# Reordering the opening of a two-branch kernel: tile 3 transposed between two half ups, its root before two gate copies, the v of tile 1 copied earlier, tile 0 normalised in two halves

## The chip, the cores and the metric

The kernel runs on one core of a Trainium2 chip. The metric is the device time of one execution in microseconds (us); the time of a kernel is the median of several executions. The engines of the core run side by side, each through its own instructions in a fixed order: TensorE (PE in the profile, with its weight loads as PEld), VectorE (DVE), ScalarE (ACT), GpSimd (POOL) and SyncE (SP), which issues the transfers.

## The reference

A token block `x` of 2048 rows and 512 columns is normalised row by row, and two branches are computed from the normalised `xn` and added to `x`:

```
xn = layernorm(x)
# branch A: linear attention, 32 heads of 16, feature map softmax(+p), softmax(-p)
q, k, v = split(xn @ wqkv)
phi_q, phi_k = features(q @ w_phi), features(k @ w_phi)
kv, z = sum over tokens of phi_k x v, sum of phi_k
A = ((phi_q @ kv) / (phi_q @ z + 1e-6)) @ wo
# branch B: gated product, F = 1792
B = ((xn @ w_gate) * (xn @ w_up)) @ w_down
out = x + A + B
```

All inputs and the output are bf16; sums are float.

## The kernel before, in words

Tokens are cut into 16 tiles of 128, and the tiles into 4 groups of 4. Everything that multiplies needs the normalised tokens transposed (columns on partitions): `xnT`, four chunks of 128 columns. From there on TensorE carries the work: v, k and q products per tile (`proj`, line 249), the gate and up products of branch B per chunk f of 128 of the 1792 hidden columns and per group (`half`, line 280; `unit`, line 297), the sums over phi_k and v (`kv`), the attention output (`attend`), and the last products `fin`. The order on each engine is written out by hand: every engine runs its instructions in the order in which the program issues them, and waits at each one for what it reads and for the buffer it writes.

The change touches the opening, lines 348 to 386, which handles the first four tiles while the weights still arrive. For a tile n of these four:

- `ln_sums(n)` (line 160): VectorE takes the statistics of the row block, once its load has landed.
- `first_std(n, ...)` (line 338): VectorE aggregates them to mean and variance (line 339), ScalarE takes the root of the variance (line 341).
- `first_apply(n)` (line 343): VectorE inverts the root (line 345) and normalises the tile (line 178, in `ln_apply`).
- `lt(n)` (line 217): TensorE transposes the tile in four pieces (line 223) into one PSUM bank (tile 0: two banks), and ScalarE copies the bank to `xnT` in two halves (line 226). `proj` reads the chunks of `xnT` in order, so it can begin behind the first half.
- `proj(pv, n, wv)`: the v product, and `vcopy(n, ...)` (line 332) moves it to SBUF, on ScalarE for tiles 0 and 1, on VectorE for 2 and 3.

Between them stand gate and up products of the first two hidden chunks for tokens 0 to 255 only (tiles 0 and 1, `2 * P` columns): g of chunks 0 and 1, then u of chunks 0 and 1. `gate_copy` (line 287) moves a gate product to SBUF on ScalarE, and `hidden` (line 292) multiplies it with the up product on VectorE. After tile 3's v product the second halves of these chunks follow (tokens 256 to 511), then full units.

PSUM results come from a pool of six banks that are handed out in turn (`bank`, line 155): a product that takes a bank waits until the bank's last reader is through. The v products of tiles 0 and 1 have banks of their own. `warm_up` (line 325) issues matmuls on constants whose result nobody reads: nine of 512 columns and one of 256 at the start, one of 512 between the transposes of tile 0 and the first v product.

SyncE issues all loads of the opening in one list (lines 84 to 101), ahead of everything else: x of tiles 0 and 1, wv in two parts, x of tile 2, gate weights of chunks 0 and 1, x of tile 3, up weights of chunks 0 and 1, and on.

Of the kernel before, what the change touches and what calls it, by code (L numbers as in the profile page):

```python
# [11 lines left out]
ALU = mybir.AluOpType  # L12
# [9 lines left out]
def kernel(  # L22
# [12 lines left out]
    nc = tc.nc  # L35
    P = 128
    S, D = A_x.shape[-2], A_x.shape[-1]
# [25 lines left out]
    xall = xpool.tile([P, NT, D], BF16)  # L63
# [44 lines left out]
    def table(func, i):  # L108
        nc.scalar.activation(out=first[:, i:i + 1], in_=ones[:, 0:1], func=func, scale=1.0)
# [45 lines left out]
    def bank(name, dt=F32, n=TT):  # L155
        return ps_s.tile([P, n], dt, name=name, tag="s")
# [3 lines left out]
    def ln_sums(n):  # L160
        stats = lnpool.tile([P, nc.vector.BN_STATS_DIM], F32, name="stats")
        nc.vector.bn_stats(out=stats[:], in_=xall[:, n, :])  # L162
        return stats
# [9 lines left out]
        nc.gpsimd.tensor_tensor(out=rstd[:, 0:k], in0=ve[:, 0:k], in1=mhalf[:, 0:k], op=ALU.pow)  # L173
        return rstd

    def ln_apply(n, mean, rstd):
        xn = xnpool.tile([P, D], BF16, name="xn")
        nc.vector.tensor_scalar(out=xn[:], in0=xall[:, n, :], scalar1=mean, scalar2=rstd,
                                op0=ALU.subtract, op1=ALU.mult)
        xns[n] = xn  # L180

    def mv_tile():
        return lnpool.tile([P, GT, nc.vector.BN_AGGR_DIM], F32, name="mv", bufs=GT)
# [33 lines left out]
    def lt(n, nbanks=1):  # L217
        step = DC // nbanks
        tps = []
        for lo in range(0, DC, step):  # L220
            tp = bank("tp", BF16).rearrange("p (c t) -> p c t", c=DC)
            for c in range(lo, lo + step):
                nc.tensor.transpose(out=tp[:, c, :], in_=xns[n][:, c * P:(c + 1) * P], identity=ident[:])  # L223
            tps.append(tp)
        for lo in range(0, DC, 2):
            nc.scalar.copy(out=xnT[:, lo:lo + 2, n * P:(n + 1) * P], in_=tps[lo // step][:, lo:lo + 2, :])  # L226
# [3 lines left out]
    def make_bd():  # L230
        bo, wp = BO[:], wphi[:]
        nc.vector.tensor_tensor(out=bd[:], in0=_bcast_ap(bo, [bo.ap[0], [0, DC], [E1, 8], [1, DH]]),
                                in1=_bcast_ap(wp, [wp.ap[0], [DH, DC], [0, 8], [1, DH]]), op=ALU.mult)
# [15 lines left out]
    def proj(ps, n, w, js=range(DC)):  # L249
        for j in js:  # L250
            nc.tensor.matmul(ps, lhsT=xnT[:, j, n * P:(n + 1) * P], rhs=w[:, j, :],  # L251
                             start=(j == 0), stop=(j == DC - 1))
# [27 lines left out]
    def half(w, name, T, f, lo, hi):  # L280
        ps = bank(name)[:, 0:hi - lo]
        for c in range(DC):
            nc.tensor.matmul(ps, lhsT=w[:, c, f * P:(f + 1) * P], rhs=xnT[:, c, T * TT + lo:T * TT + hi],  # L283
                             start=(c == 0), stop=(c == DC - 1))
        return ps

    def gate_copy(ps, n):
        g_sb = gpool.tile([P, TT], BF16, name="g_sb")
        nc.scalar.copy(out=g_sb[:, 0:n], in_=ps)  # L289
        return g_sb  # L290

    def hidden(T, f, ps, g_sb, lo, hi):
        if T not in hTs:
            hTs[T] = hpool.tile([P, FC, TT], BF16, name="hT", tag="h")
        nc.vector.tensor_tensor(out=hTs[T][:, f, lo:hi], in0=ps, in1=g_sb[:, 0:hi - lo], op=ALU.mult)  # L295
# [29 lines left out]
    def warm_up(k, n=TT):  # L325
        for _ in range(k):
            nc.tensor.matmul(warm[:, 0:n], lhsT=ones[:, 0:P], rhs=ones[:, 0:n], start=True, stop=True)  # L327
# [4 lines left out]
    def vcopy(n, ps, copy=nc.scalar.copy):  # L332
        copy(out=vts[n % NV][:, :, :, 0:DH], in_=ps.rearrange("p (a b c) -> p a b c", a=8, b=4))  # L333

    mvs = [mv_tile() for n in range(GT)]
    stds = {}

    def first_std(n, stats):
        nc.vector.bn_aggr(out=mvs[n][:, 0, :], in_=stats[:])
        stds[n] = lnpool.tile([P, 1], F32, name="std", bufs=GT)  # L340
        nc.scalar.activation(out=stds[n][:], in_=mvs[n][:, 0, 1:2], func=AF.Sqrt, bias=epst[:], scale=1.0)

    def first_apply(n):
        rstd = lnpool.tile([P, 1], F32, name="rs1", bufs=GT)
        nc.vector.reciprocal(out=rstd[:], in_=stds[n][:])
        ln_apply(n, mvs[n][:, 0, 0:1], rstd[:])

    with tc.tile_pool(name="ps_v", bufs=1, space=PSUM) as ps_v:
        pv = [ps_v.tile([P, D], F32, name=f"pv{n}") for n in range(2)]
        first_std(0, ln_sums(0))  # L350
        stats = ln_sums(1)
        first_apply(0)
        first_std(1, stats)
        first_apply(1)
        lt(0, nbanks=2)
        warm_up(1)
        proj(pv[0][:], 0, wv, range(2))
        lt(1)
        proj(pv[0][:], 0, wv, range(2, DC))
        proj(pv[1][:], 1, wv)  # L360
        first_std(2, ln_sums(2))
        first_apply(2)
        vcopy(0, pv[0])
        g = [half(wg, "g", 0, 0, 0, 2 * P)]
        lt(2)
        g.append(half(wg, "g", 0, 1, 0, 2 * P))
        pv2 = bank("pv")
        proj(pv2, 2, wv)
        stats = ln_sums(3)
        g_sb = [gate_copy(g[0], 2 * P)]  # L370
        first_std(3, stats)
        first_apply(3)
        g_sb.append(gate_copy(g[1], 2 * P))
        vcopy(1, pv[1])
        u0 = half(wu, "u", 0, 0, 0, 2 * P)
        hidden(0, 0, u0, g_sb[0], 0, 2 * P)
        vcopy(2, pv2, nc.vector.tensor_copy)
        u1 = half(wu, "u", 0, 1, 0, 2 * P)
        hidden(0, 1, u1, g_sb[1], 0, 2 * P)
        lt(3)  # L380
        pv3 = bank("pv")
        proj(pv3, 3, wv)
        make_bd()
        vcopy(3, pv3, nc.vector.tensor_copy)
        table(AF.Exp, 1)
        nc.gpsimd.tensor_tensor(out=M4[:], in0=BO[:, 0:4, :], in1=BO[:, 4:8, :], op=ALU.add)
# [141 lines left out]
```

## Time and profile before

| | |
|---|---|
| median of 3 executions | 222.68 us (222.62 to 222.80) |
| the profiled execution, own time | 222.58 us |
| its span in the profile | 220.9 us |
| TensorE busy | 216.7 us (98%), 1309 matmuls |
| VectorE, ScalarE, GpSimd busy | 138.7, 89.4, 68.8 us |
| HBM read, written | 8.67 MB, 2.10 MB |

The span runs from the first instruction to the last; what lies around it is part of the time but not of the trace. In the views by time a row has the start and the length of a run of like instructions, in us from the start of the span, then engine, line, operation, what it writes and reads, and in brackets how long the engine stood idle before it and what ended that. Matmuls overlap: a row ends when the last result is out, some time after the array could take the next one, so the pace is read from start to start. In the view by stretches the columns are the stretch and its length, busy time and number of instructions for PE, PEld, DVE, ACT and POOL, then the granted clock of TensorE, the share of the DMA engines and their GB/s. In the view by groups the last column is busy time in us and the mean length of one in ns, then the idle time before.

### The profile page before, as it was taken

What the parts mean: (1) busy time and instruction counts of PE and PEld (TensorE: products, weight loads), DVE (VectorE), ACT (ScalarE), POOL (GpSimd) and SP (SyncE); (2) the same over time, 40 slices, a digit from 0 to 9 for tenths busy, and PEclk for the clock granted to TensorE, in tenths of its full rate; (3) what the DMA queues carried; (4) which work ended last, traced back from release to release, by engine and by line L of the source; (5) the groups of instructions that cost most, each with busy time, mean ns of one, the idle gap of its engine ahead of it and who ended that gap; (6) DMA issues with size and microseconds to landing.
All of it is one profiled execution on the core that took longest, in us unless ns stands there. A gap on an engine that the chain in (4) does not pass through costs nothing.

```text
span 220.9 us, 3515 instructions
## 1 busy us (share of the span) xinstructions
PE 216.7 (98%) x1309; PEld 104.7 (47%) x1309; DVE 138.7 (63%) x241; ACT 89.4 (40%) x170; POOL 68.8 (31%) x54
## 2 busy tenths in 40 slices
PE   8999999999999999999999999999999999999994
PEld 3554444445444444444444444444444444454443
DVE  4657986785569785757489964097645745444321
ACT  3665575449764885546353221231322323100000
POOL 3000455546335653637333643024033033000000
PEclk9999999999999999999999999999999999999999
DMA  6999985502310324020204945214431431522501
GB/s 191 227 306 391 363 215 73 96 0 46 29 22 8 57 42 85 5 45 1 47 3 91 122 99 107 64 24 95 98 71 24 95 74 24 91 53 71 71 27 48
DMA packets 47249, 19.91 MB, mean 90 GB/s; under 512 B 37504, under 2 KB 46976, under 8 KB 47104
## 3 DMA queue, kind: packets, MB, share of 16 engines
q1 hardware_dynamic: 47232, 19.69, 39.5%
q8 instruction: 10, 0.16, 0.3%
q14 instruction: 7, 0.06, 0.1%
HBM read 8.67 MB, written 2.10 MB: 49 GB/s over the span
## 4 chain that ended last, share of the span: by engine, by line
PE 98%; ACT 0%; DVE 0%; issue 0%
PE g L283 22%; PE fin L313 22%; PE u L283 22%; PE pv L251 7%; PE fin L316 6%; PE k L251 6%; PE q L251 6%; PE warm L327 2%; PE ab L471 2%; PE kv L406 2%; PE pq L242 1%; PE tp L223 1%; ACT xnT L226 0%; DVE o_sb L319 0%
## 5 line engine op out<-in xcount | busy, mean ns | idle before, releaser
L283 PE MATMUL g<-xnT,wg 128*128 128x512 bf16 (+1 forms) x232 | 57.8, 372 | 0.0
L283 PE MATMUL u<-xnT,wu 128*128 128x512 bf16 (+1 forms) x232 | 57.7, 372 | 0.0
L295 DVE TENSOR_TENSOR hT<-u,g_sb 128x512 bf16<-128x512 f32 (+1 forms) x58 | 37.2, 649 | 26.2 <-PE u L283 15.1
L264 DVE TENSOR_REDUCE sums<-e 128x64 f32<-128x1024 f32 x32 | 38.9, 1216 | 21.5 <-ACT e L261 21.5
L289 ACT CAST g_sb<-g 128x512 bf16<-128x512 f32 (+1 forms) x58 | 33.4, 576 | 45.4 <-PE g L283 44.8
L313 PE MATMUL fin<-wd,hT 128*128 128x512 bf16 (+2 forms) x238 | 51.1, 366 | 0.0
L268 POOL TENSOR_TENSOR phiq<-e,rs 128x1024 bf16<-128x1024 f32 x16 | 30.9, 1933 | 60.8 <-DVE rs L266 53.6
L268 POOL TENSOR_TENSOR phik<-e,rs 128x1024 bf16<-128x1024 f32 x16 | 30.9, 1932 | 55.6 <-DVE rs L266 44.1
L283 PEld LDWEIGHTS <-wu 128*128 128x128 bf16 x232 | 22.7, 98 | 25.9
L313 PEld LDWEIGHTS <-hT 128*128 128x128 bf16 x238 | 22.4, 98 | 24.7
L283 PEld LDWEIGHTS <-wg 128*128 128x128 bf16 x232 | 21.9, 98 | 23.4 <-DMA wg<-in_B_w_gate_dram 0.2
L251 PEld LDWEIGHTS <-xnT 128*128 128x128 bf16 x192 | 17.2, 97 | 19.2 <-ACT xnT L226 2.4
L319 DVE TENSOR_TENSOR o_sb<-fin,xall 128x512 bf16<-128x512 f32 (+2 forms) x17 | 11.2, 656 | 22.3 <-PE fin L316 22.2
L251 PE MATMUL pv<-wv,xnT 128*128 128x512 bf16 x64 | 22.5, 380 | 0.5 <-ACT xnT L226 0.5
L251 PE MATMUL k<-W1k,xnT 128*128 128x512 bf16 x64 | 22.3, 379 | 0.0
L260 ACT ACTIVATE e<-q 128x512 f32<-128x512 f32 x16 | 9.5, 596 | 25.4 <-PE q L251 25.4
L266 DVE RECIPROCAL rs<-sums 128x64 f32<-128x64 f32 x32 | 17.7, 553 | 3.1
L316 PE MATMUL fin<-wo,oT 128*128 128x512 bf16 (+2 forms) x68 | 16.6, 366 | 0.0
L251 PE MATMUL q<-W1q,xnT 128*128 128x512 bf16 x64 | 16.4, 378 | 0.0
L333 ACT CAST vt<-pv 128x512 bf16<-128x512 f32 x14 | 8.3, 590 | 17.4 <-PE pv L251 17.4
L162 DVE BATCH_NORM_STATS2 stats<-xall 128x6 f32<-128x512 bf16 x16 | 10.7, 668 | 1.3 <-DMA xall<-in_A_x_dram 1.3
L480 DVE TENSOR_TENSOR otok<-ab,rden 128x512 bf16<-128x512 f32 x16 | 11.1, 692 | 0.6
(48 smaller groups left out, 117.7 us busy)
## 6 DMA issues: line engine op xcount, KB each, us to landing
out_dram<-o_sb SPq DMA_DIRECT2D x15, 128.0 KB, 2.0
wd<-in_B_w_down_dram SPq DMA_DIRECT2D x1, 1792.0 KB, 15.8
wg<-in_B_w_gate_dram SPq DMA_DIRECT2D x2, 640.0 KB, 6.9
wu<-in_B_w_up_dram SPq DMA_DIRECT2D x2, 640.0 KB, 8.2
xall<-in_A_x_dram SPq DMA_DIRECT2D x1, 1024.0 KB, 12.2
xall<-in_A_x_dram SPq DMA_DIRECT2D x4, 128.0 KB, 2.6
wv<-in_A_wqkv_dram SPq DMA_DIRECT2D x2, 256.0 KB, 3.0
wg<-in_B_w_gate_dram SPq DMA_DIRECT2D x2, 256.0 KB, 4.8
```

The costliest lines, as they stand in the source:

```text
L162: nc.vector.bn_stats(out=stats[:], in_=xall[:, n, :])
L251: nc.tensor.matmul(ps, lhsT=xnT[:, j, n * P:(n + 1) * P], rhs=w[:, j, :], start=(j == 0), stop=(j == DC - 1))
L264: nc.vector.tensor_reduce(out=sums[:], in_=ev, axis=AX.X, op=ALU.add)
L266: nc.vector.reciprocal(out=rs[:].rearrange("p a b -> p (a b)"), in_=sums[:])
L268: nc.gpsimd.tensor_tensor(out=phi[:].rearrange("p g (x f) -> p (g x) f", f=DH), in0=ev, in1=rs[:].to_broadcast((P, 2 * H, DH)), op=ALU.mult)
L283: nc.tensor.matmul(ps, lhsT=w[:, c, f * P:(f + 1) * P], rhs=xnT[:, c, T * TT + lo:T * TT + hi], start=(c == 0), stop=(c == DC - 1))
L289: nc.scalar.copy(out=g_sb[:, 0:n], in_=ps)
L295: nc.vector.tensor_tensor(out=hTs[T][:, f, lo:hi], in0=ps, in1=g_sb[:, 0:hi - lo], op=ALU.mult)
L313: nc.tensor.matmul(ps, lhsT=hTs[T][:, f, t4 * P:(t4 + 1) * P], rhs=wd[:, f, lo:lo + w], start=(f == 0), stop=False)
L316: nc.tensor.matmul(ps, lhsT=oTs[n][:, c, :], rhs=wo[:, c, lo:lo + w], start=False, stop=(c == DC - 1))
L319: nc.vector.tensor_tensor(out=o_sb[:], in0=ps, in1=xall[:, n, lo:lo + w], op=ALU.add)
L480: nc.vector.tensor_tensor(out=o_tok[:].rearrange("p (b h d) -> p b h d", b=2, d=DH), in0=abv[:, :, :, 0:DH], in1=rden[:].to_broadcast((P, ...
```

## The change

Four edits, all in the opening:

1. Tile 0 is normalised in two passes of 256 columns instead of one of 512 (`parts=2`), and the warm-up product between its transposes and the first v product has 256 columns instead of 512.
2. The v of tile 1 is copied by ScalarE right behind that of tile 0, ahead of tile 2's transposes and their copies; before, it came behind both gate copies.
3. On ScalarE the root of tile 3 comes ahead of both gate copies; before, it stood between them.
4. On TensorE tile 3 is transposed between the two half up products; before, behind both. With that its PSUM bank and that of the second up product change places in the turn, and ScalarE and VectorE get their copies and `hidden` in the matching order.

```diff
-    def ln_apply(n, mean, rstd):
+    def ln_apply(n, mean, rstd, parts=1):
         xn = xnpool.tile([P, D], BF16, name="xn")
-        nc.vector.tensor_scalar(out=xn[:], in0=xall[:, n, :], scalar1=mean, scalar2=rstd,
-                                op0=ALU.subtract, op1=ALU.mult)
+        for lo in range(0, D, D // parts):
+            hi = lo + D // parts
+            nc.vector.tensor_scalar(out=xn[:, lo:hi], in0=xall[:, n, lo:hi], scalar1=mean, scalar2=rstd,
+                                    op0=ALU.subtract, op1=ALU.mult)
         xns[n] = xn
...
-    def first_apply(n):
+    def first_apply(n, parts=1):
         rstd = lnpool.tile([P, 1], F32, name="rs1", bufs=GT)
         nc.vector.reciprocal(out=rstd[:], in_=stds[n][:])
-        ln_apply(n, mvs[n][:, 0, 0:1], rstd[:])
+        ln_apply(n, mvs[n][:, 0, 0:1], rstd[:], parts)
...
-        first_apply(0)
+        first_apply(0, 2)
         first_std(1, stats)
         first_apply(1)
         lt(0, nbanks=2)
-        warm_up(1)
+        warm_up(1, 2 * P)
...
         vcopy(0, pv[0])
+        vcopy(1, pv[1])
         g = [half(wg, "g", 0, 0, 0, 2 * P)]
         lt(2)
         g.append(half(wg, "g", 0, 1, 0, 2 * P))
         pv2 = bank("pv")
         proj(pv2, 2, wv)
-        stats = ln_sums(3)
-        g_sb = [gate_copy(g[0], 2 * P)]
-        first_std(3, stats)
+        first_std(3, ln_sums(3))
         first_apply(3)
-        g_sb.append(gate_copy(g[1], 2 * P))
-        vcopy(1, pv[1])
+        g_sb = [gate_copy(ps, 2 * P) for ps in g]
         u0 = half(wu, "u", 0, 0, 0, 2 * P)
         hidden(0, 0, u0, g_sb[0], 0, 2 * P)
         vcopy(2, pv2, nc.vector.tensor_copy)
+        lt(3)
         u1 = half(wu, "u", 0, 1, 0, 2 * P)
         hidden(0, 1, u1, g_sb[1], 0, 2 * P)
-        lt(3)
         pv3 = bank("pv")
         proj(pv3, 3, wv)
```

## The prediction

> **What bounds the kernel now.** I read the page's totals and its chain that ended last first, then the busy time by stretches, then the opening on TensorE, its weight loads (PEld), VectorE and ScalarE.
>
> ```profile
> PE 216.7 (98%) x1309; PEld 104.7 (47%) x1309; DVE 138.7 (63%) x241; ACT 89.4 (40%) x170; POOL 68.8 (31%) x54
> ...
> PE 98%; ACT 0%; DVE 0%; issue 0%
> ```
> ```profile
> 11.00:12.00 1.00, 0.54 (x7) 0.35 (x6) 1.00 (x3) 0.53 (x2) 0.00 (x0) 1.00 1.28 290
> ...
> 17.00:60.00 43.00, 43.00 (x269) 20.49 (x270) 31.75 (x52) 27.84 (x51) 17.91 (x16) 1.00 0.58 151
> ...
> 120.00:215.00 95.00, 95.00 (x538) 45.16 (x538) 53.51 (x93) 18.07 (x33) 19.33 (x10) 1.00 0.37 71
> ```
> TensorE sets the end: from 17 to 215 us it has work in every microsecond, so whatever reaches the matmul stream earlier there ends earlier by as much. The holes are in the opening. All the edits lie there, before the second-half gate products that start at 12.77, and the question is how much earlier those start.
>
> ```profile
> 4.99 0.61 PE L223 MATMUL tp<-ident,xn 128*128 128x128 bf16 x4
> 5.39 0.57 PE L327 MATMUL warm<-const-bfloat16-1.0 128*128 128x512 bf16 x1
> 5.85 0.60 PE L251 MATMUL pv<-wv,xnT 128*128 128x512 bf16 x2
> 6.29 0.39 PE L223 MATMUL tp<-ident,xn 128*128 128x128 bf16 x4
> ...
> 8.01 0.60 PE L283 MATMUL g<-xnT,wg 128*128 128x256 bf16 x4
> 8.45 0.39 PE L223 MATMUL tp<-ident,xn 128*128 128x128 bf16 x4
> 8.67 0.60 PE L283 MATMUL g<-xnT,wg 128*128 128x256 bf16 x4
> 9.30 1.04 PE L251 MATMUL pv<-wv,xnT 128*128 128x512 bf16 x4
> 10.18 1.04 PE L283 MATMUL u<-xnT,wu 128*128 128x256 bf16 x8
> 11.05 0.39 PE L223 MATMUL tp<-ident,xn 128*128 128x128 bf16 x4
> 11.90 1.04 PE L251 MATMUL pv<-wv,xnT 128*128 128x512 bf16 x4 [0.47 <-ACT xnT L226]
> 12.77 0.60 PE L283 MATMUL g<-xnT,wg 128*128 128x256 bf16 x4
> ```
> ```profile
> 5.84 0.11 PEld L251 LDWEIGHTS <-xnT 128*128 128x128 bf16 x2 [0.41 <-ACT xnT L226]
> ...
> 7.14 0.11 PEld L251 LDWEIGHTS <-xnT 128*128 128x128 bf16 x2 [0.52 <-ACT xnT L226]
> ...
> 7.83 0.50 PEld L283 LDWEIGHTS <-wg 128*128 128x128 bf16 x4 [0.15 <-DMA wg<-in_B_w_gate_dram]
> ...
> 11.90 0.11 PEld L251 LDWEIGHTS <-xnT 128*128 128x128 bf16 x2 [0.64 <-ACT xnT L226]
> ```
> From the starts: four transposes occupy TensorE for 0.22 (8.45 to 8.67), four 256-column products 0.435 (8 from 10.18 to 11.05), four 512-column ones 0.87 (11.90 to 12.77). The last result comes out 0.16 after the array is free (10.34 against 10.18). So tile 3's transposes leave the array at 11.27 and the v product of tile 3 waits until 11.90: 0.63 empty, the largest hole. The first v product (5.85) and that of tile 1 (7.14) wait for copies too.
>
> ```profile
> 4.52 0.41 DVE L178 TENSOR_SCALAR xn<-xall,mv,rs 128x512 bf16<-128x512 bf16 x1
> 4.85 0.18 DVE L339 BATCH_NORM_AGGREGATE mv<-stats 128x2 f32<-128x6 f32 x1
> ...
> 5.59 0.41 DVE L178 TENSOR_SCALAR xn<-xall,mv,rs 128x512 bf16<-128x512 bf16 x1
> ...
> 8.96 0.18 DVE L339 BATCH_NORM_AGGREGATE mv<-stats 128x2 f32<-128x6 f32 x1
> ...
> 10.22 0.41 DVE L178 TENSOR_SCALAR xn<-xall,mv,rs 128x512 bf16<-128x512 bf16 x1
> ```
> ```profile
> 5.06 0.30 ACT L341 ACTIVATE std<-mv,epst 128x1 f32<-128x1 f32 x1 [0.89 <-DVE mv L339]
> 5.42 0.65 ACT L226 COPY xnT<-tp 128x256 bf16<-128x256 bf16 x2
> ...
> 8.87 0.65 ACT L226 COPY xnT<-tp 128x256 bf16<-128x256 bf16 x2 [0.84 <-PE tp L223]
> 9.41 0.39 ACT L289 CAST g_sb<-g 128x256 bf16<-128x256 f32 x1
> 9.67 0.32 ACT L341 ACTIVATE std<-mv,epst 128x1 f32<-128x1 f32 x1
> 9.87 0.38 ACT L289 CAST g_sb<-g 128x256 bf16<-128x256 f32 x1
> 10.12 0.62 ACT L333 CAST vt<-pv 128x512 bf16<-128x512 f32 x1
> 11.47 0.65 ACT L226 COPY xnT<-tp 128x256 bf16<-128x256 bf16 x2 [0.73 <-PE tp L223]
> ```
> Steps that I use below: normalised tile to transposes 0.06 (4.52 + 0.41 to 4.99); first transpose to copy 0.42 (11.05 to 11.47); copy 0.375 (two in 0.65, the second 0.27 behind) and then 0.05 to the weight load at 11.90; a root to the next ScalarE instruction 0.20 (9.67 to 9.87); a pass over a tile to the next VectorE instruction 0.33 (4.52 to 4.85).
>
> **Tile 0 in two halves (one VectorE instruction more).** No row shows a half pass. Two rows bound it from near:
>
> ```profile
> L295 DVE TENSOR_TENSOR hT<-u,g_sb 128x256 bf16<-128x256 f32 x4 | 1.7, 422 | 0.9 <-ACT g_sb L289 0.7 <-PE u L283 0.2
> ...
> L476 DVE TENSOR_SCALAR den<-ab 128x32 f32<-128x32 f32 x16 | 2.9, 180 | 0.0
> ```
> The same operation with 32 columns takes 0.18, of which some 0.15 is fixed if a float column costs 1 ns. That leaves 0.26 of the 0.41 for 512 columns, and half of it, 0.13, is what a half saves: 0.28 long, with 0.20 to the next. The ends: nothing fixed (0.21 long, 0.165 to the next) and nothing saved (0.41, 0.33). With 0.28 the first half ends at 4.80, its transposes start at 4.86 instead of 4.99 and the copy could start at 5.29. But the second half starts at 4.72, tile 1's aggregate at 4.92 instead of 4.85 and its root at 5.13; the root stands before the copy on ScalarE, so the copy starts at 5.33, against 5.42: **0.09 gained**. At the good end the copy is bound by the transposes, which wait for the last warm-up product (array free at about 4.83), and 0.14 is gained; at the bad end the root slips by 0.33, the copy starts at 5.59 and 0.17 is lost. I take 0.09, since the 32-column row is the same operation.
>
> The Trainium skill, VectorE: DVE Perf Modes, "The perf-mode tier table", speaks against it: it lets such an operation on bf16 in SBUF move four columns a cycle, so that 512 columns would take an estimated 0.13 and a half would save 0.07. The measured 0.41 with a fixed 0.15 fits half that rate; by the page the copy would start at 5.45 and the edit would lose 0.03.
>
> The 0.09 is handed on. Tile 1's normalised tile, pushed by 0.07 to 5.66, is ready at 6.13 and wanted at 6.20; its v product moves from 7.14 to 7.05; the first gate product from 8.01 to 7.92. That needs wg, whose wait ended at 7.83: 0.09 of slack is left, and if it is gone the 0.09 is lost again there.
>
> **The shorter warm-up product** costs nothing: the half-width one ends by about 5.5, and TensorE then waits for the copy anyway (now 0.41). What it might do to the pace is a rival below.
>
> **v of tile 1 ahead of tile 2's copies.** The product's last result is out at 7.92 + 0.16; the copy runs from 8.11, and with the full 0.62 of its row ScalarE is free at 8.73. Tile 2's transposes move from 8.45 to 8.36, so their copies are due at 8.78. Hidden, by 0.05 at the worst; beyond that each 0.1 delays tile 2's v product by 0.1.
>
> **Root of tile 3 ahead of both gate copies.** Its aggregate ends at 9.14 (8.96 + 0.18), unchanged. ScalarE is free of tile 2's copies at 9.32 (where the gate copy stood at 9.41, less 0.09), so the root starts at 9.32, 0.35 earlier than 9.67, and tile 3 is normalised from 9.87 and ready at 10.34. The gate copies follow at about 9.52 and 9.78 and end by 10.2. Who waits for them: the first `hidden`, not before 10.7, and the bank of the first gate product, wanted again at 10.75. Both covered.
>
> **Transposes of tile 3 between the halves.** The first up half runs from 10.09 to 10.53; the transposes need 10.34 (0.19 of slack), run to 10.75, and the second up half to 11.18. Copies: 10.53 + 0.42 = 10.95, out at 11.32, v product of tile 3 at 11.37 instead of 11.90. The second up half covers 0.435 of the wait and 0.19 of 0.63 stays: **0.44 gained**. The second hidden product ends only slightly earlier than now, since VectorE still has the v of tile 2 before it; its bank is wanted at about 14.0, two microseconds later.
>
> Sum: 0.09 + 0.44 = 0.53; the gate products of the second half start at 12.24 instead of 12.77. The only thing that could take this back is what comes by the clock on the wall rather than by TensorE: the loads.
>
> ```profile
> 11.48 0.50 SPq L78 DMA_DIRECT2D wu<-in_B_w_up_dram  x1
> ...
> DMA to landing us min/median/max: 6.2/6.2/6.2
> ...
> 19.52 1.03 PE L283 MATMUL u<-xnT,wu 128*128 128x512 bf16 x4
> ```
> This load of up weights lands at 17.7 and is first read by the product at 19.52 (19.0 afterwards): 1.3 stays. No DMA is issued earlier or later by the change. So 0.53 should reach the end: the profiled execution (span 220.9, its own time 222.58) would go to 222.05, and the median 222.68, 0.10 above it, to **222.15**.
>
> **Rivals.** (a) The opening gains nothing: a half pass costs nearly as much as a whole one, or wg is late. The 0.44 stays: 222.68 - 0.44 = 222.24; at the worst bound (0.17 lost) 222.41. For it: no half pass in the trace, 0.09 of slack at wg. Against it: the 32-column row.
> (b) The wait moves and does not shrink: the root of tile 3 is held as now, its tile is ready at 10.22 + 0.47 = 10.69, the transposes wait 0.16 and the gain is 0.37: 222.31. Against it: ScalarE's order then has nothing in front of the root but copies that end earlier.
> (c) Slower: the matmul pace. The granted clock reads 1.00 throughout, but the ten warm-up products keep half pace:
>
> ```profile
> 0.83 4.21 PE L327 MATMUL warm<-const-bfloat16-1.0 128*128 128x512 bf16 x10 [0.83 <-PEq L512]
> ```
> Nine and a half in about 4.0 us are about 0.42 each; the first v products take 0.22 (5.85 to 6.29). The pace doubles between the last transpose and 5.85. The change thins out the work just before that: where the array is now empty for about 0.2 us, it would be for about 0.4 (a gap between the transpose pairs, and 5.5 to 5.76). Should the doubling fail there and need as long a dense run again (0.83 to 4.83, 4.0 us), TensorE would run at half pace to 9.76 and lose 2.0, less some 0.4 of holes that it fills: 1.6 - 0.53 = 1.1 slower, 223.8. It decides wherever the first v products come at 0.43. Against it: nine tenths of those microseconds stay busy.
> The Trainium skill, TensorE: Matmul & The Clock Gate, "What's actually happening", has the clock watched in free-running windows of 3.4 us; by it a missed window costs an estimated 1.7 - 0.4 - 0.53, about 0.8, so 223.5. That its windows also wander from run to run is not borne out: the three runs lie within 0.18.
>
> **How the numbers follow.** Chances: the forecast 0.60, (a) 0.20, (b) 0.08, (c) 0.07, an unknown stall 0.05. A measurement of this kernel tells about 0.2%, 0.45 us, from no change, so the forecast of 0.53 is only just beyond it. Faster: most of the forecast and a little of (a), 0.58. Same: the rest of these and (b), 0.32. Slower: (c) and half of the unknown, 0.10. The range: below, the good end of the half pass (0.05 more) and 0.15 for the spread of the runs, 221.95; above, the worst of (a) and (b) with 0.14 for that spread, 222.55.
>
> **What would show it.** Right: the first xnT copy near 5.33, the root of tile 3 near 9.32 and ahead of both gate copies, tile 3's transposes near 10.5 with no wait, the v product of tile 3 at about 11.4 behind a hole of 0.2, the next gate product at 12.2, and everything later earlier by the same half microsecond. Wrong: a wait ahead of tile 3's transposes, first v products 0.43 apart, a wait for wg that grows, or a copy of tile 2 that starts after 8.8.

## The result and the profile after

| | before | after |
|---|---|---|
| median | 222.59 us (222.46 to 222.98, 22 executions) | 222.22 us (222.05 to 223.01, 22 executions) |
| ratio of the times | | 0.9984, 95% interval 0.9977 to 0.9990 |
| profiled execution: span, own time | 220.9, 222.58 us | 220.5, 222.24 us |

The change gains 0.16%, 0.36 us of 222.6, with an interval of 0.22 to 0.51. The forecast was 0.53 and 222.15; the time lies inside the range, and the gain is nearer to the 0.44 of rival (a) than to 0.53.

The opening on TensorE in the kernel after, by the view in order of time (start, length, operation):

```profile
0.82 3.72 PE L329 MATMUL warm<-const-bfloat16-1.0 128*128 128x512 bf16 x10 [0.82 <-PEq L512]
4.91 0.54 PE L225 MATMUL tp<-ident,xn 128*128 128x128 bf16 x4 [0.37 <-DVE xn L180]
...
5.84 0.60 PE L253 MATMUL pv<-wv,xnT 128*128 128x512 bf16 x2 [0.28 <-ACT xnT L228]
...
8.11 0.61 PE L285 MATMUL g<-xnT,wg 128*128 128x256 bf16 x4
...
10.28 0.60 PE L285 MATMUL u<-xnT,wu 128*128 128x256 bf16 x4
10.71 0.39 PE L225 MATMUL tp<-ident,xn 128*128 128x128 bf16 x4
10.94 0.60 PE L285 MATMUL u<-xnT,wu 128*128 128x256 bf16 x4
11.56 1.04 PE L253 MATMUL pv<-wv,xnT 128*128 128x512 bf16 x4
12.44 0.60 PE L285 MATMUL g<-xnT,wg 128*128 128x256 bf16 x4
```

Its weight loads, which carry the waits in brackets:

```profile
8.10 0.33 PEld L285 LDWEIGHTS <-wg 128*128 128x128 bf16 x4 [0.42 <-DMA wg<-in_B_w_gate_dram]
...
11.56 0.11 PEld L253 LDWEIGHTS <-xnT 128*128 128x128 bf16 x2 [0.30 <-ACT xnT L228]
```

Two readings. From the first up product to the v product of tile 3 it was 1.72 (10.18 to 11.90); now it is 1.28 (10.28 to 11.56). That is the 0.44 of the moved transposes, to the hundredth. But the first up product itself is no earlier: 10.28 against 10.18. The first v product starts at 5.84, as before (5.85), and the first gate product is even later (8.11 against 8.01) because its weights landed later in this execution.

VectorE and ScalarE show why the first copy gained nothing. First VectorE in order of time, then its groups by shape (busy us, mean ns of one), then ScalarE in order of time:

```profile
4.51 0.60 DVE L180 TENSOR_SCALAR xn<-xall,mv,rs 128x256 bf16<-128x256 bf16 x2
5.03 0.17 DVE L341 BATCH_NORM_AGGREGATE mv<-stats 128x2 f32<-128x6 f32 x1
```
```profile
L180 DVE TENSOR_SCALAR xn<-xall,mv,rs 128x512 bf16<-128x512 bf16 x3 | 1.2, 412 | 0.1
...
L180 DVE TENSOR_SCALAR xn<-xall,mv,rs 128x256 bf16<-128x256 bf16 x2 | 0.6, 343 | 0.0
```
```profile
5.24 0.29 ACT L343 ACTIVATE std<-mv,epst 128x1 f32<-128x1 f32 x1 [1.07 <-DVE mv L341]
5.44 0.62 ACT L228 COPY xnT<-tp 128x256 bf16<-128x256 bf16 x2
...
8.21 0.59 ACT L335 CAST vt<-pv 128x512 bf16<-128x512 f32 x1 [0.18 <-PE pv L253]
8.98 0.65 ACT L228 COPY xnT<-tp 128x256 bf16<-128x256 bf16 x2 [0.18 <-PE tp L225]
9.51 0.31 ACT L343 ACTIVATE std<-mv,epst 128x1 f32<-128x1 f32 x1
9.70 0.65 ACT L291 CAST g_sb<-g 128x256 bf16<-128x256 f32 x2
```

A half pass takes 0.343, a whole one 0.412: half the columns save 0.069, not 0.13 (the group of two covers both halves of tile 0). So the two halves push tile 1's aggregate from 4.85 to 5.03 and its root from 5.06 to 5.24, and the first copy, next on ScalarE 0.20 later, starts at 5.44 against 5.42. The remaining edits of ScalarE's order went as forecast: the v of tile 1 is through at 8.80, before the copies of tile 2 at 8.98, and the root of tile 3 follows these copies directly, at 9.51.

### The profile page after: what moved, and what is told of

It is laid out like the page before. It is cut to its first block, busy times and chain, and to the rows that moved or that the text cites. A ratio compares the mean times of both kernels' runs of the same rounds, so it can differ in the third digit from the quotient of the medians.

```text
span 220.5 us, 3517 instructions
## 1 busy us (share of the span) xinstructions
PE 216.1 (98%) x1309; PEld 104.4 (47%) x1309; DVE 138.9 (63%) x242; ACT 89.4 (41%) x170; POOL 68.8 (31%) x54
## 4 chain that ended last, share of the span: by engine, by line
PE 96%; DVE 1%; DMA 1%; ACT 0%; issue 0%
PE g L285 22%; PE fin L315 22%; PE u L285 22%; PE pv L253 7%; PE fin L318 6%; PE q L253 6%; PE k L253 6%; PE ab L471 2%; PE kv L406 2%; DMA xall<-in_A_x_dram 1%; PE pq L244 1%; DVE stats L162 1%; PE tp L225 0%; DVE xn L180 0%; ACT std L343 0%
```

## The experiments

All numbers of this table are starts in the profiled execution of each kernel, in us; "stretch" is from the first up product to the v product of tile 3, "second halves" the first gate product of tokens 256 to 511. Ratios are to the kernel before, run beside it, with 95% intervals. They come from four series: the result; e1 to e4; e5 to e9; a2 and e11 to e13. The kernel before had medians of 222.59, 222.64, 222.80 and 222.63 in them, so a ratio of one series is compared with one of another only with care. A ratio is good to about 0.1%, 0.2 us, so what is worth a few hundredths is read from the traces, one execution of each kernel.

| kernel | first copy | first up | v of tile 3 | stretch | second halves | span | median | ratio |
|---|---|---|---|---|---|---|---|---|
| before | 5.42 | 10.18 | 11.90 | 1.72 | 12.77 | 220.9 | | |
| after | 5.44 | 10.28 | 11.56 | 1.28 | 12.44 | 220.5 | 222.22 | 0.9984 (0.9977 to 0.9990) |
| a2_after | 5.48 | 10.22 | 11.51 | 1.29 | 12.38 | 220.5 | 222.45 | 0.9989 (0.9979 to 0.9999) |
| e1_whole | 5.33 | 10.88 | 12.17 | 1.29 | 13.04 | 221.1 | 222.24 | 0.9983 (0.9974 to 0.9993) |
| e2_halves_only | 5.37 | 10.11 | 11.83 | 1.72 | 12.71 | 220.8 | 222.88 | 1.0004 (0.9993 to 1.0015) |
| e3_old_act | 5.41 | 10.67 | 12.04 | 1.37 | 12.92 | 221.0 | 222.35 | 0.9990 (0.9980 to 1.0000) |
| e4_act_only | 5.43 | 10.21 | 11.93 | 1.72 | 12.81 | 220.9 | 222.82 | 1.0004 (0.9991 to 1.0017) |
| e5_agg_between | 5.39 | 10.15 | 11.44 | 1.29 | 12.31 | 220.4 | 222.19 | 0.9980 (0.9966 to 0.9994) |
| e7_agg_wg | 5.29 | 10.22 | 11.51 | 1.29 | 12.38 | 220.5 | 222.17 | 0.9971 (0.9959 to 0.9983) |
| e8_x2_early | 5.48 | 10.51 | 11.79 | 1.28 | 12.67 | 220.8 | 222.46 | 0.9977 (0.9966 to 0.9988) |
| e9_all | 5.40 | 10.39 | 11.68 | 1.29 | 12.55 | 220.7 | 222.35 | 0.9975 (0.9965 to 0.9984) |
| e11_root1_first | 5.26 | 10.02 | 11.30 | 1.28 | 12.18 | 220.3 | 222.02 | 0.9972 (0.9961 to 0.9983) |
| e12_root1_whole | 5.33 | 10.09 | 11.38 | 1.29 | 12.25 | 220.4 | 222.16 | 0.9981 (0.9971 to 0.9990) |
| e13_root1_wg | 5.29 | 10.04 | 11.34 | 1.30 | 12.21 | 220.3 | 222.11 | 0.9975 (0.9965 to 0.9986) |

One thing is seen at once: span less the start of the second halves is 208.1, to within a tenth, in every row (220.9 - 12.77, 221.1 - 13.04, 220.3 - 12.18). Whatever the opening does arrives at the end in full in these executions, and nothing after it gives or takes.

### The parts one by one

Without the half passes (`e1_whole`):

```diff
-        first_apply(0, 2)
+        first_apply(0)
...
-        warm_up(1, 2 * P)
+        warm_up(1)
```

> The change without its first part: tile 0 is normalised in one pass of 512 columns and the warm-up product has 512 columns again; the other three edits stay. Theory H (the profile after: two half passes took 0.60 together against 0.41 for the whole, so the first copy of xnT started no earlier): this is as fast as the changed kernel or up to 0.03 us faster, 0.36 to 0.40 us under the kernel before; the first copy of xnT at 5.42, the v product of tile 3 about 1.28 behind the first up product. Rival P (the prediction: the halves gain 0.09 and something else took it back): 0.09 slower than the changed kernel, 0.27 under the kernel before.

The half passes alone (`e2_halves_only`): the kernel before with

```diff
-        first_apply(0)
+        first_apply(0, 2)
...
-        warm_up(1)
+        warm_up(1, 2 * P)
```

> The kernel before with the first part of the change alone: tile 0 in two half passes, warm-up product of 256 columns; tile 3, the roots and the v copies as before. Theory H: no gain, between 0.03 slower and 0.02 faster than before; tile 1's aggregate about 0.18 later than with one pass (5.03 against 4.85), its root at 5.24, the first copy of xnT at 5.44. Rival P: 0.09 faster than before, the copy at 5.33.

The kernel after with ScalarE's old order (`e3_old_act`):

```diff
-        vcopy(1, pv[1])
         g = [half(wg, "g", 0, 0, 0, 2 * P)]
...
-        first_std(3, ln_sums(3))
+        stats = ln_sums(3)
+        g_sb = [gate_copy(g[0], 2 * P)]
+        first_std(3, stats)
         first_apply(3)
-        g_sb = [gate_copy(ps, 2 * P) for ps in g]
+        g_sb.append(gate_copy(g[1], 2 * P))
+        vcopy(1, pv[1])
```

> The changed kernel with ScalarE's old order: gate copy 0, root of tile 3, gate copy 1, v of tile 1. Tile 3's transposes stay between the half ups. Theory W (the root's early place is worth little): the root comes 0.26 later than in the changed kernel, tile 3 is ready about 0.3 later, its transposes wait under 0.1, and of the 0.44 of the moved transposes 0.35 to 0.40 stay; the time is 0.05 to 0.09 above that of the changed kernel. Rival (b) of the prediction: the transposes wait 0.16 and only 0.28 stays. If the v copy of tile 1, now right before the copies of tile 3, holds these up, the v product of tile 3 starts later than 1.35 behind the first up product.

The kernel before with only ScalarE's new order (`e4_act_only`), that is, the kernel after in which tile 0 is whole and

```diff
-        lt(3)
         u1 = half(wu, "u", 0, 1, 0, 2 * P)
         hidden(0, 1, u1, g_sb[1], 0, 2 * P)
+        lt(3)
```

> The kernel before with only ScalarE's new order: v of tile 1 early, root of tile 3 ahead of both gate copies; tile 0 in one pass, tile 3 transposed behind both half ups. Theory M (all of the gain is TensorE's moved transposes): 0, within 0.05 of the kernel before; the hole of 0.63 ahead of tile 3's v product stays, though tile 3 is normalised about 0.3 earlier. Rival: the order on ScalarE carries part of the gain, 0.1 or more faster.

By the times, the halves are worth nothing that a ratio can show: 0.9983 without them and 0.9984 with them, 1.0004 when they come alone. The same holds for ScalarE's order alone (1.0004). The traces say more. The half passes alone, in order of time, VectorE and ScalarE:

```profile
4.45 0.60 DVE L180 TENSOR_SCALAR xn<-xall,mv,rs 128x256 bf16<-128x256 bf16 x2
4.96 0.17 DVE L341 BATCH_NORM_AGGREGATE mv<-stats 128x2 f32<-128x6 f32 x1
```
```profile
5.17 0.29 ACT L343 ACTIVATE std<-mv,epst 128x1 f32<-128x1 f32 x1 [1.08 <-DVE mv L341]
5.37 0.62 ACT L228 COPY xnT<-tp 128x256 bf16<-128x256 bf16 x2
```

Everything is 0.07 earlier here, since x of tile 0 landed earlier (the pass starts at 4.45, not 4.52). Counted from the start of the pass, the aggregate comes after 0.51 and the copy after 0.92; before it was 0.33 and 0.90. Theory H holds: the root is 0.18 later, and the copy 0.02.

The 0.02 depends on the pace at which TensorE ran in the profile of before. There the four transposes of tile 0 took 0.40 from start to start (4.99 to 5.39), and the copy came 0.43 behind the first. In `e1_whole`, also with one pass, they took 0.24 and the copy came 0.32 behind the first:

```profile
4.54 0.41 DVE L180 TENSOR_SCALAR xn<-xall,mv,rs 128x512 bf16<-128x512 bf16 x1
...
5.01 0.40 PE L225 MATMUL tp<-ident,xn 128*128 128x128 bf16 x4 [0.69 <-DVE xn L180]
...
5.25 0.38 PE L329 MATMUL warm<-const-bfloat16-1.0 128*128 128x512 bf16 x1
...
5.33 0.65 ACT L228 COPY xnT<-tp 128x256 bf16<-128x256 bf16 x2
```

So from the start of the pass to the copy it is 0.90 in one and 0.79 in the other. With two halves and the root behind them it is 0.92 or 0.93 in all five profiles (the kernel after twice, `e2_halves_only`, `e3_old_act`, `e8_x2_early`), because there the root holds the copy and not TensorE. Set against one pass, the halves therefore cost 0.02 at the pace of before and 0.14 where the pace has doubled earlier; the times are too coarse to show either.

With the old order on ScalarE the weight load for tile 3's transposes does wait:

```profile
11.18 0.23 PEld L225 LDWEIGHTS <-xn 128*128 128x128 bf16 x4 [0.19 <-DVE xn L180]
```

In the kernel after this load ran 0.10 ahead of its matmul (10.61 and 10.71), so only part of the 0.19 shows: the stretch is 1.37, 0.09 more than 1.28, at the upper edge of theory W. The v copy of tile 1, back in its old place, is not the cause: ScalarE stood idle for 0.39 before it copied tile 3. So the early root is worth 0.09, and the transposes by themselves 0.35; without the moved transposes the early root buys nothing (1.72 in `e4_act_only`). Moving the v copy cost and gained nothing that any of these traces shows; no run moves it alone.

### What holds the opening besides: the loads

`e1_whole` starts its first copy at 5.33, earlier than the kernel after, and still ends later in its profile (221.1). VectorE and TensorE of that execution:

```profile
7.21 0.69 DVE L162 BATCH_NORM_STATS2 stats<-xall 128x6 f32<-128x512 bf16 x1 [1.19 <-DMA xall<-in_A_x_dram]
```
```profile
9.15 0.40 PE L225 MATMUL tp<-ident,xn 128*128 128x128 bf16 x4 [0.42 <-DVE xn L180]
```

The statistics of tile 2 waited 1.19 for x and began at 7.21, against 5.91 in the profile of before; tile 2's transposes are 0.7 late (9.15 against 8.45). The same is seen in `e3_old_act` (first up product at 10.67). The executions of most kernels spread by such amounts: the kernel before took between 222.50 and 223.67 in one series of 35. Two experiments moved loads: x of tile 2 between the parts of wv (`e8_x2_early`), and the first gate load in two (`e7_agg_wg`, which contains `e5_agg_between`: tile 1's aggregate and root between the two half passes). `e9_all` does all three.

```diff
     for lo in (0, 2):
         nc.sync.dma_start(out=wv[:, lo:lo + 2, :],
...
-    dma_x(2, 3)
+        if lo == 0:
+            dma_x(2, 3)
```

> The changed kernel with x of tile 2 issued between the two parts of wv instead of behind both. Theory X (the runs of each kernel lie in two groups some 0.6 apart because x of tile 2 lands anywhere from 5.7 to 7.2 and holds tile 2 when it lands after about 6.5): the landing moves to under 6.2, the upper group thins out, and the median falls by up to 0.1; the fastest runs do not change. Rival: the second part of wv then lands after 6.5 and holds tile 0's v product: 0.1 to 0.3 slower. Rival 2: the upper group has another cause and stays.

```diff
+            if between is not None and lo == 0:
+                between()
...
-        first_apply(0, 2)
-        first_std(1, stats)
+        first_apply(0, 2, lambda: first_std(1, stats))
```

> The changed kernel with one order changed on VectorE and ScalarE: tile 1's aggregate (and its root) comes between the two half passes of tile 0 instead of behind both. Theory H2 (the halves gained nothing because tile 1's aggregate, and with it its root in front of the first copy on ScalarE, slipped by 0.18): the root comes near 5.0, the first copy of xnT near 5.25 instead of 5.44, the first v product near 5.65. What is left of that at the end depends on wg: its load lands near 7.8 to 8.1 and the first gate product, then due at 7.85, waits for it, so the time is 0 to 0.15 under the changed kernel. Rival: the copy is held by the transposes themselves and stays at 5.4.

```diff
-    dma_cols(nc.sync, wg, B_w_gate, 0, 2 * P)
+    dma_cols(nc.sync, wg, B_w_gate, 0, P)
+    dma_cols(nc.sync, wg, B_w_gate, P, 2 * P)
```

> As e5_agg_between, and the first gate load is cut in two, one of 128 columns for chunk 0 and one for chunk 1. Theory L (the first gate product is held by the load of wg): chunk 0 lands about 0.3 before the whole did, the wait there goes and 0.1 to 0.2 is won against the changed kernel. Rival: the smaller rows (256 bytes) slow the queue, later loads slip, and it is the same or slower.

> The changed kernel with all three: tile 1's aggregate between the half passes, the first gate load cut in two, x of tile 2 between the parts of wv. If H2, L and X hold, 0.15 to 0.25 under the changed kernel, 0.5 to 0.6 under the kernel before, and with a narrower spread. If the loads push each other, it lies between e7_agg_wg and e8_x2_early.

With x of tile 2 early, the twelve executions of `e8_x2_early` lie between 222.17 and 222.81, where those of `e5_agg_between` beside it reach from 221.89 to 223.28: the late tail is missing, and so is the fast end. Its ratio, 0.9977, is not told from that of the kernel after. TensorE of that kernel shows the first rival: the second part of wv is now the late one.

```profile
6.93 1.24 PE L254 MATMUL pv<-wv,xnT 128*128 128x512 bf16 x5 [0.22 <-DMA wv<-in_A_wqkv_dram]
```

`e5_agg_between` had its root at 5.03 as expected, but the first copy at 5.39, not 5.25: there the rival was right, the transposes held it. They ran at the slow pace in that execution (four from 4.96 to 5.47, the second half pass from 4.91), and the copy came 0.43 behind the first, as before. In `e7_agg_wg` the first gate product did not wait for wg, but tile 2 did for x, whose statistics waited 0.72; in `e9_all` the first two v products were 0.4 apart, at the slow pace. Its ratio, 0.9975, lies between those of `e7_agg_wg` and `e8_x2_early`, and all three are within each other's intervals, so the times do not decide its case.

Theory L is not borne out. Chunk 0 by itself landed 3.8, 4.5 and 4.3 after its issue (`e7_agg_wg`, `e9_all`, `e13_root1_wg`), the whole load 3.8 to 5.1 in the other eleven profiles; the waits for wg differ from execution to execution without any cut (none in `a2_after`, 0.42 in the kernel after); `e7_agg_wg` has the median of `e5_agg_between` (222.17 and 222.19), and `e13_root1_wg` below does not beat `e11_root1_first`. What the traces show is that one load or another was late in several of these executions: x of tile 2 in `e1_whole`, `e3_old_act` and `e7_agg_wg`, wg in the kernel after, `e1_whole`, `e2_halves_only` and `e8_x2_early`, wv in `e8_x2_early`. That moving one load ahead makes another late rests on the one profile of `e8_x2_early`.

### The slipped root taken away

`a2_after` is the kernel after once more. The last three, run beside it, put tile 1's aggregate between tile 0's reciprocal and its pass. There it takes little of VectorE's time: from the reciprocal to the pass it is 0.22 (4.35 to 4.57 in `e11_root1_first`) instead of 0.18 (4.33 to 4.51 in the kernel after).

```diff
         nc.vector.reciprocal(out=rstd[:], in_=stds[n][:])
+        if ahead is not None:
+            ahead()
...
-        first_apply(0, 2)
-        first_std(1, stats)
+        first_apply(0, 2, lambda: first_std(1, stats))
```

This is `e11_root1_first`. `e12_root1_whole` does it with one pass over tile 0 and the warm-up product of 512 columns, `e13_root1_wg` with the first gate load cut in two.

> The changed kernel once more, beside the three that follow. Theory D (the time up to the first up product goes by the landing of the loads, and differs from execution to execution; behind it the stretch from the first up product to tile 3's v product is fixed): that stretch is 1.28 again, against 1.72 before, whatever the loads do, and the ratio to the kernel before is 0.998 to 0.999. Rival: the stretch itself varies.

> The changed kernel with tile 1's aggregate (and its root) between the reciprocal of tile 0 and its two half passes. Theory H3 (with the root out of the way, a half pass is worth the 0.065 by which it is shorter than a whole one, and no more): tile 1's root near 4.65, the first half ends near 4.89, the first copy of xnT starts 0.05 to 0.10 before that of e12_root1_whole at the same pace of the warm-up products; the time is 0 to 0.15 under the changed kernel, as the loads allow. Rival: the half is worth 0.13 (first copy near 5.25), as the prediction had it.

> As e11_root1_first with tile 0 in one pass and the warm-up product of 512 columns. Theory H3: tile 1's root near 4.65, the whole pass ends near 4.95, the first copy of xnT at 5.35 to 5.45; the time within 0.1 of e11_root1_first.

> As e11_root1_first, and the first gate load cut in two, chunk 0 by itself. Theory L: chunk 0 lands near 7.0 to 7.7 and the first gate product does not wait for it; 0.1 to 0.2 under the changed kernel, 0.5 under the kernel before, if x of tile 2 lands by 6.3. Rival: x of tile 2 and tile 3 land later by the cut and hold their tiles, and it is not faster than e11_root1_first.

ScalarE of the kernel after (its second profile), of `e11_root1_first` with half passes, and of `e12_root1_whole` with one pass:

```profile
5.28 0.29 ACT L343 ACTIVATE std<-mv,epst 128x1 f32<-128x1 f32 x1 [1.07 <-DVE mv L341]
5.48 0.63 ACT L228 COPY xnT<-tp 128x256 bf16<-128x256 bf16 x2
```
```profile
4.68 0.29 ACT L343 ACTIVATE std<-mv,epst 128x1 f32<-128x1 f32 x1 [0.50 <-DVE mv L341]
5.26 0.65 ACT L228 COPY xnT<-tp 128x256 bf16<-128x256 bf16 x2 [0.28 <-PE tp L225]
```
```profile
4.69 0.29 ACT L343 ACTIVATE std<-mv,epst 128x1 f32<-128x1 f32 x1 [0.50 <-DVE mv L341]
5.33 0.65 ACT L228 COPY xnT<-tp 128x256 bf16<-128x256 bf16 x2 [0.35 <-PE tp L225]
```

The releaser changes: in the kernel after the copy simply follows the root, in the other two it waits for the transposes. With the root gone from in front of it the copy is 0.22 earlier (5.48 to 5.26), and now the half pass is worth 0.07 over the whole one (5.33 to 5.26), which is its measured 0.069 and not 0.13. The copy's 5.26 is the figure that the rival named, but the whole pass came earlier too, at 5.33 and not 5.42, since the transposes ran at full pace in both profiles (the copy 0.32 behind the first one, 4.94 to 5.26 and 5.01 to 5.33); so the difference decides, and it is 0.07. In these two profiles x of tile 2 and wg were not late for their tiles, and the 0.07 arrives in full: second halves at 12.18 and 12.25. Against `a2_after` (12.38) `e11_root1_first` gains 0.20 in its profile. It has the lowest median of the study, 222.02, beside 222.45 for the kernel after in the same series, and 0.9972 (0.9961 to 0.9983) of the kernel before, 0.6 us. The intervals of these two ratios overlap slightly, but five of its six executions (221.96 to 222.10) lie below all eleven of `a2_after` (222.15 and up). It is not told from `e13_root1_wg` (0.9975), or from `e7_agg_wg` (0.9971) in another series.

## Why the prediction came out as it did

**Right: the transposes between the halves.** 0.44 forecast, 0.44 measured in the profile (1.72 to 1.28), and 0.42 to 0.44 in every kernel that has the edit with the early root, whatever its loads did. The hole that stays is 0.19 (array free at 11.38, product at 11.56), as worked out.

**Right: the root's early place is its cover; the size was 0.09 and not 0.16.** With it the transposes of tile 3 had the 0.19 of slack that was forecast (tile ready at 10.05 + 0.47, transposes at 10.71). Without it rival (b) had 0.16 of waiting; `e3_old_act` loses 0.09. The difference lies in the half pass: the 0.16 counted on a first up product 0.09 earlier, which did not come.

**Right: the v of tile 1, the bank turn, the gate copies.** All hidden. The copy of tile 1's v ends 0.18 before that of tile 2 starts in the first profile, where the gate product between them waited for wg, and 0.07 in the second (8.26 + 0.59 to 8.92), close to the forecast's worst case of 0.05.

**Wrong: the half pass, "0.09 gained".** The step that failed is the term for the half pass, 0.13 saved by a half and with it "I take 0.09, since the 32-column row is the same operation". A half saves 0.069, and 0.27 of a pass is fixed if the columns cost the same throughout (0.343 for 256 columns less another 0.069). The 32-column row shared the operation's name but read float from PSUM and had a constant where the pass has two values per partition; taking its 0.15 for fixed was the error. Which of these differences makes the fixed part larger was not tried. The rule quoted there from the Trainium skill, VectorE: DVE Perf Modes, "The perf-mode tier table", gave 0.07 for a half and a root that makes the copy 0.03 late; measured were 0.069 and 0.02. The trace agrees with the page in what a half saves, and the sentence that set it aside was mistaken. So rival (a) is what happened: 0.44 less 0.02, about 0.42, at the pace of the profile of before. The profile's 0.33 (12.77 to 12.44) is this less the 0.09 or so that the first gate product came later because its weights landed late in that execution. The second profile, with wg in time, has 0.39. The measured interval, 0.22 to 0.51, holds 0.42 and just leaves out 0.53. That the time itself, 222.22, is only 0.07 above the forecast is in part luck: the forecast counted from 222.68, and the kernel before took 222.59 beside it.

A second figure of the same step fitted by chance. The 0.42 from the first transpose to the copy was read from tile 3, whose bank takes four transposes. A bank of tile 0 takes two, and at full pace its copy came 0.32 behind the first (`e1_whole`, `e11_root1_first`, `e12_root1_whole`); it was 0.43 in the profile of before because its transposes ran at the slow pace.

**Wrong in a side remark: the pace.** The prediction said that the wandering of the clock's windows was not borne out. The moment at which the pace doubles does wander. The ten warm-up products took 4.21 in the profile before, 3.72 in the one after and this in `e1_whole`:

```profile
0.83 3.49 PE L329 MATMUL warm<-const-bfloat16-1.0 128*128 128x512 bf16 x10 [0.83 <-PEq L512]
```

So the pace doubled before the end of these products in some executions, and in others only after the first v product had begun:

```profile
5.83 0.84 PE L257 MATMUL pv<-wv,xnT 128*128 128x512 bf16 x2
```

That is `e9_all`: two products in 0.84 where the others need 0.60. This agrees with the Trainium skill, TensorE: Matmul & The Clock Gate, "What's actually happening". That three runs of before agree to 0.18 does not speak against it: where the pace doubles early, TensorE is done with these products sooner and waits for the normalised tile (0.37 idle in the kernel after, 0.69 in `e1_whole`), so little of it reaches the end. What the doubling does to the time was not measured by itself. Rival (c) did not happen: with less work in front of them the first v products of the kernel after start 0.23 apart.

**Not seen beforehand: the loads.** The prediction looked for loads that become late because TensorE comes earlier, and found 0.09 of slack at wg. That x of tile 2 lands 3.0 after its issue in one execution (the profile of before) and 4.5 in another (`e1_whole`) could not be read from one profile; in `e1_whole` tile 2 came 0.7 late by it, more than the whole change.

## What to carry to other kernels

A pass cut in two pays its fixed part twice, and whatever stands behind it on its engine pays for that: look first for what is queued behind the pass, and move it ahead, before cutting. Filling a hole in the bounding engine with work of its own is worth the length of that work, up to the length of the hole; here the second up product filled 0.44 of 0.63. What the moved work reads must be ready early enough, so move what prepares it in the same edit. The fixed part of an instruction is read from the same kind of operands, not from the same name.

## What the runs showed that was not expected

Executions of one kernel differ by more than 0.5 us for most kernels here, and late loads in the opening are one cause that the profiles show: the statistics of tile 2 could start at 5.91 in one profile and had to wait until 7.21 in another. And the pace of the matmuls doubles at a time that differs by about two microseconds between executions (warm-up products of 3.49 to 4.21, and once not before 5.83), while the granted clock of these stretches reads 1.00 at both paces, so the pace has to be read from start to start.
